# Linear-attention state of a fused kernel: the fade of the old state done on TensorE into PSUM, and the sum copied out by ScalarE

## Chip, core and metric

One Trainium2 chip, one core. The metric is the time of one execution on the device in microseconds (us), as the median of some runs. The reader needs four of the core's engines: PE (TensorE, matrix products into PSUM), DVE (VectorE), ACT (ScalarE) and POOL (GpSimd); SP issues the transfers (DMAs) between HBM and SBUF.

## What is computed

A linear attention with a decaying state, followed by two products with gating and a second block with softmax and normalisation. Only the first part matters here. In the reference, per block of rows and per head:

```python
inter = np.einsum('bhid,bhde->bhie', qb * lam_pow[None], kv_state)
out[:, :, sl] = intra + inter
kb_dec = kb * rev_pow[None]
kv_state = lam_block[None, :, None, None] * kv_state + np.einsum('bhsd,bhse->bhde', kb_dec, vb)
```

The state of a head is 64 x 64. It is faded by one number per head, `lam_block`, and a product of decayed keys and values is added. There are 2 batches, 8 heads, 768 positions, head size 64; then 1536 rows go through 512 x 1536 (twice), 1536 x 512, 512 x 1024 and 1024 x 512.

## The kernel before

The attention runs over 12 chunks of 128 positions, numbered n = 0 to 11: batch n % 2, position n // 2. Chunk n needs the state that chunk n - 2 left (`state[n - B]`, B = 2). Chunks 10 and 11 are the last of their batch, so ten states are made, the first two (n = 0, 1) without an old one.

A state is one SBUF tile of 128 partitions x 4 x 64 in fp32: eight heads as four pairs `a`, head `e` = 0 of a pair in partitions 0 to 63 and head 1 in partitions 64 to 127. `dec` holds the powers of the decay of each head, in the same layout; its last column, `dec[:, :, P - 1]`, is the decay over a whole chunk.

Every step of the work is a Python generator, and every `yield` ends a part of it. The table `ORDER` lists the parts one by one in the order in which they are issued (`T,5` a second time is the second part of `T` for chunk 5), and each engine runs what it is given in that order. So a row of the table sets the place in the queue of every engine that the part uses. The kinds that matter here:

- `A` (`scores`): products of queries and keys (`pss`, L223), then the mask on DVE (`sc`, L228).
- `K`, `Q` (`kdecay`, `qdecay`): decayed keys `kd` (L208) and queries `qd` (L214), on POOL.
- `C` (`products`): eight products of the old state with `qd` (`px`, L238), eight of values with `sc` (L244), and a maximum on DVE (L114).
- `O` (`fade`): POOL multiplies the old state by the decay of the chunk, into a tile `old` (L254).
- `T` (`carry`): first part eight products of `kd` and values into a PSUM bank `pst` (L263); second part a DVE addition of `old` and `pst` into a new state (L269), or, for n = 0 and 1, a copy by ACT (L267).
- `X`, `Y`, `J`: scales and splits of `px` into half-precision pairs (L123 on PE, L131 to L134, L297, L313 on DVE, L293, L319 on ACT).
- `D`, `S`: weights decoded (ACT L340, L344, DVE L346) and split into `wab` (ACT L418, DVE L421).
- `L`, `R`: the first products of the second stage (L143, out `pa`, `pb` and `rA`, `rB`, `rC`).

All PSUM banks come from one ring of eight. Tiles `state` and `old` share a ring of four. The products in fp32 show as two records on PE each, so a set of eight is x16 in the profile.

Of the kernel before, what the change touches and what calls it, by code (L numbers as in the profile page):

```python
# [8 lines left out]
F32 = mybir.dt.float32  # L9
# [8 lines left out]
B, H, S, D = 2, 8, 768, 64  # L18
P = 128
W = 512  # L20
WARM = 22
NP = H // 2
# [7 lines left out]
NJ = W // P  # L30

LAST = 2
ORDER = ("G,qk,0 G,kv,0 G,qk,1 G,ab,0 G,kv,1 G,qk,2 G,kv,2 G,qk,3 G,kv,3 G,ab,1 G,qk,4 G,kv,4 G,qk,5 G,kv,5 A,0 K,0 K,0 A,0 T,0 A,0 C,0 T,0 O,2 A,1 C,0 D,ab,0 "
# [59 lines left out]
def body(ctx: ExitStack, tc, qk, kv, consts, wab, wo, wi, wo2, out):  # L93
    nc = tc.nc
    E = mybir.EngineType
    ctx.enter_context(tc.manual_schedule(engines={E.SP, E.PE, E.DVE, E.Activation, E.Pool}))
    const = ctx.enter_context(tc.tile_pool(name="const", bufs=1))
    sl = ctx.enter_context(tc.tile_pool(name="sl", bufs=1))
# [3 lines left out]
    def bank(nm):  # L102
        return ps.tile([P, W], F32, tag="bank", name=nm)
# [64 lines left out]
    dec = const.tile([P, NP, P], F32, name="dec")  # L168
# [5 lines left out]
    ident = const.tile([P, P], F32, name="ident")  # L174
# [17 lines left out]
    n = 1  # L192
# [2 lines left out]
        n *= 2  # L195


    order = [(g % B, g // B) for g in range(NCH)]
    sc, qd, kd, px, state = {}, {}, {}, {}, {}
    xs, sx, xst, olds = {}, {}, {}, {}  # L200

    def kdecay(n):

# [44 lines left out]
        amax(xst[n // 2][:, n % 2:n % 2 + 1], o)  # L248
        yield

    def fade(n):
        b, c = order[n]
        olds[n] = sl.tile([P, NP, D], F32, tag="state", name="old", bufs=4)
        nc.gpsimd.tensor_mul(olds[n], state[n - B], dec[:, :, P - 1:P].to_broadcast([P, NP, D]))  # L254
        yield

    def carry(n):
        b, c = order[n]
        v = kvs[n][:, 1]
        pst = bank("pst")[:, :NP * D].rearrange("p (a d) -> p a d", a=NP)  # L260
        for a in range(NP):
            for e in range(2):
                nc.tensor.matmul(pst[e * D:(e + 1) * D, a], kd[n][:, 2 * a + e], v[:, 2 * a + e], start=True, stop=True, skip_group_check=True)  # L263
        yield
        new = sl.tile([P, NP, D], F32, tag="state", name="state", bufs=4)
        if c == 0:
            nc.scalar.copy(new, pst)  # L267
        else:
            nc.vector.tensor_add(new, olds[n], pst)  # L269
        state[n] = new  # L270
        yield

# [574 lines left out]
    def load(nm, n):  # L847
# [4 lines left out]
        else:  # L852
            load_w((nm, n))
        yield

    kinds = {"G": load, "A": scores, "K": kdecay, "Q": qdecay, "C": products, "O": fade, "T": carry, "X": scale_x, "Y": split_x,
             "D": decode, "P": scale_w, "p": scale_f, "S": split_w, "J": sums_x, "H": sums_w, "E": split_s, "R": R1, "L": L1, "M": L2, "U": scale_y, "V": split_y, "B": sums_y, "F": split_ys, "I": sums_i, "k": split_si, "N": L3, "n": norm, "Z": Z, "W": L4}
    parts = {}
    for word in ORDER.split():
        if word not in parts:  # L860
# [48 lines left out]
```

## Time and profile before

| | |
|---|---|
| median of 3 runs | 457.61 us (457.37 to 458.52) |
| the profiled execution's own time | 457.83 us |
| its span, first to last instruction | 456.1 us |
| PE busy | 438.5 us of the span |
| DVE, ACT, POOL busy | 337.7, 248.5, 232.2 us |
| granted TensorE clock, mean | 0.981 |

The profile is one execution taken by the hardware profiler. Its time outside the span is 1.73 us. Attention work stands in the first 125 us or so, mixed with the first products of the second stage; from then on PE runs the large products. Three views are used below: the chain of work that ended last, followed back from the last instruction; the timeline, with an engine's idle time before a group in brackets and who ended it; and a table of stretches with the busy time of each engine in each and the granted clock of PE (1.00 is 2.4 GHz, 0.50 is 1.2 GHz).

### The profile page before, as it was taken

The page shows a single profiled execution, that of the slowest core. Times are in us where ns is not written, and L with a number is a line of the kernel's source. Part 1 is how long each engine was busy: PE and PEld are TensorE (multiplying, and loading weights), DVE is VectorE, ACT ScalarE, POOL GpSimd, SP SyncE. Part 2 cuts the span into 40 slices and gives each one's busy share as a digit, 9 for nine tenths or more (in the row PEclk, how much of TensorE's full clock was granted, in tenths as well). Part 3 has the DMA queues.
Part 4 walks back from the last instruction along what each step waited for, and adds up shares of the span by engine and source line. Part 5 has one row for each costly group of instructions (what it writes and reads, how often), then busy time and mean ns, then how long its engine had stood idle before and what let it go on. Part 6 is the DMA issues. An engine that isn't in the chain of part 4 may idle for free.

```text
span 456.1 us, 7817 instructions
## 1 busy us (share of the span) xinstructions
PE 438.5 (96%) x3092; PEld 273.9 (60%) x3092; DVE 337.7 (74%) x571; ACT 248.5 (54%) x397; POOL 232.2 (51%) x259
## 2 busy tenths in 40 slices
PE   6879699999999999999999999999999989999997
PEld 5768565457888886776874444455444434444455
DVE  5798889899887446556699259977986879996830
ACT  2473636677776556556884526756714645534321
POOL 4796534595615652152526247338244794837500
PEclk9879889999999999999999999999999999999999
DMA  8957418552200004340222422020012123344511
GB/s 309 416 200 279 185 59 311 185 184 94 93 1 0 2 1 161 125 177 1 93 92 86 192 96 91 0 94 1 2 23 46 48 38 78 70 115 105 127 47 46
DMA packets 30372, 48.74 MB, mean 107 GB/s; under 512 B 22272, under 2 KB 22528, under 8 KB 27008
## 3 DMA queue, kind: packets, MB, share of 16 engines
q1 hardware_dynamic: 30336, 48.25, 31.2%
q8 instruction: 24, 0.39, 0.4%
q14 instruction: 12, 0.10, 0.1%
HBM read 39.86 MB, written 3.15 MB: 94 GB/s over the span
## 4 chain that ended last, share of the span: by engine, by line
PE 86%; DMA 4%; POOL 4%; DVE 2%; ACT 1%; issue 1%; SPq 0%; ACTq 0%; POOLq 0%
PE py L143 20%; PE rA L143 14%; PE po L143 13%; PE pa L143 7%; PE rB L143 7%; PE pb L143 7%; PE hA L143 5%; DMA qk<-in_qk_dram 4%; PE rC L143 3%; PE hB L143 2%; PE pss L223 2%; PE px L238 2%; PE px L244 1%; PE hC L143 1%; PE pst L263 1%
## 5 line engine op out<-in xcount | busy, mean ns | idle before, releaser
L143 PE MATMUL py<-g,wo 128*128 128x512 f16 x432 | 94.4, 379 | 0.0
L143 PEld LDWEIGHTS <-wab 128*128 128x128 f16 x744 | 72.0, 98 | 36.0 <-issue 0.9
L143 PEld LDWEIGHTS <-wo 128*128 128x128 f16 x432 | 42.1, 98 | 50.5
L143 PE MATMUL po<-wo,zT 128*128 128x512 f16 (+1 forms) x312 | 63.4, 363 | 0.0
L143 PEld LDWEIGHTS <-ws 128*128 128x128 f16 x576 | 56.0, 98 | 7.4 <-DVE ws L452 0.3
L143 PEld LDWEIGHTS <-zT 128*128 128x128 f16 x312 | 30.5, 98 | 31.5
L556 POOL TENSOR_TENSOR g<-c,g 128x512 f16<-128x512 f32 x24 | 31.2, 1318 | 33.9 <-ACT g L554 33.8
L143 PE MATMUL rA<-xt,ws 128*128 128x256 f16 x288 | 35.2, 273 | 0.0
L489 POOL TENSOR_TENSOR g<-asb,g 128x512 f16<-128x512 f32 x12 | 16.0, 1334 | 34.2 <-ACT g L487 34.2
L143 PE MATMUL pa<-xh,wab 128*128 128x512 f16 (+1 forms) x156 | 33.3, 363 | 0.0
L143 PE MATMUL pb<-xh,wab 128*128 128x512 f16 (+1 forms) x156 | 33.2, 363 | 0.0
L512 ACT ACTIVATE p<-rA 128x512 f32<-128x512 f32 x36 | 21.2, 595 | 20.6 <-PE rA L143 20.6
L800 POOL TENSOR_TENSOR zr<-e,zr 128x512 f16<-128x512 f32 x20 | 24.7, 1255 | 12.0 <-ACT zr L796 12.0
L344 ACT ACTIVATE raw<-raw 128x1024 f32<-128x1024 f32 x26 | 29.4, 1141 | 0.0
L841 ACT ACTIVATE ob<-po,glm 128x512 f32<-128x512 f32 (+1 forms) x13 | 8.4, 654 | 36.2 <-PE po L143 30.4
L545 POOL TENSOR_TENSOR c<-p,p 128x512 f32<-128x512 f32 x12 | 15.7, 1306 | 20.6 <-ACT p L512 19.5
L143 PEld LDWEIGHTS <-yt 128*128 128x128 f16 x144 | 14.0, 98 | 16.9 <-DVE yt L644 0.3
L550 DVE SCALAR_TENSOR_TENSOR c<-c 128x512 f32<-128x512 f32 x24 | 20.1, 847 | 4.9 <-ACT c L547 4.6
L346 DVE SCALAR_TENSOR_TENSOR fab<-raw,fab 128x1024 uint32<-128x1024 uint32 x12 | 15.5, 1294 | 7.4 <-ACT raw L344 7.4
L418 ACT ACTIVATE wab<-fab,sab 128x512 f16<-128x512 f32 (+1 forms) x24 | 14.4, 640 | 11.0 <-DVE sab L134 11.0
L421 DVE SCALAR_TENSOR_TENSOR wab<-fab,sab,wab 128x512 f16<-128x512 f32 (+1 forms) x24 | 18.9, 822 | 1.1 <-ACT wab L418 1.1
L796 ACT CAST zr<-e 128x512 f16<-128x512 f32 x20 | 11.4, 616 | 14.2 <-DVE e L785 14.2
(167 smaller groups left out, 902.3 us busy)
## 6 DMA issues: line engine op xcount, KB each, us to landing
raw<-in_wab_dram SPq DMA_DIRECT2D x12, 1024.0 KB, 5.5
raw<-in_wo_dram SPq DMA_DIRECT2D x10, 1024.0 KB, 4.8
qk<-in_qk_dram SPq DMA_DIRECT2D x12, 512.0 KB, 9.1
kv<-in_kv_dram SPq DMA_DIRECT2D x12, 512.0 KB, 9.9
raw<-in_wi_dram SPq DMA_DIRECT2D x4, 1024.0 KB, 5.5
out_dram<-ob SPq DMA_DIRECT2D x11, 256.0 KB, 2.0
zT<-zr SPq DMA_TRANSPOSE x20, 3.1
out_dram<-ob SPq DMA_DIRECT2D x2, 128.0 KB, 1.7
```

What stands on the lines that cost most here:

```text
L143: nc.tensor.matmul(o, w[a], x[b], start=start and i == 0, stop=stop and i == 2, skip_group_check=True)
L344: nc.scalar.activation(hi.bitcast(F32), hi.bitcast(F32), AF.Prelu, scale=2.0 ** -112, alpha=2.0 ** 32)
L346: nc.vector.scalar_tensor_tensor(out=flat, in0=hi, scalar=3, in1=flat, op0=ALU.logical_shift_left, op1=ALU.bitwise_or)
L418: nc.scalar.activation(w[:, z, 0, c], src[:, z, c], AF.Copy, scale=ss[:, z:z + 1])
L421: nc.vector.scalar_tensor_tensor(out=w[:, z, 1, c], in0=src[:, z, c], scalar=ss[:, z:z + 1], in1=w[:, z, 0, c], op0=ALU.mult, op1=ALU.subt ...
L489: nc.gpsimd.tensor_sub(g[:, 1], a, g[:, 0])
L512: nc.scalar.activation(r, o, AF.Copy, scale=2.0 ** -28)
L545: nc.gpsimd.tensor_sub(c1[:, 1], p167, p5)
L550: nc.vector.scalar_tensor_tensor(out=c[:, :, 0], in0=c[:, :, 0], scalar=2.0, in1=c[:, :, 1], op0=ALU.mult, op1=ALU.mult)
L556: nc.gpsimd.tensor_sub(g[:, 1], c[:, :, 0], g[:, 0])
L796: nc.scalar.copy(rows[0][:, z * W:(z + 1) * W], e[z])
L800: nc.gpsimd.tensor_sub(lo, e[z], hi)
```

## The change

The step `O` is gone, with its eight entries in `ORDER` and its tiles `old`. In its place a constant tile `fades` is made once, by two POOL instructions after `dec`: for every head a 64 x 64 diagonal matrix with the decay of the chunk on the diagonal. In the second part of `T`, for n = 2 to 9, eight products of this diagonal with the old state are added to `pst` in PSUM; then ACT copies the sum into the new state, where DVE added before. All other entries of `ORDER` keep their sequence.

```diff
+    fades = const.tile([P, NP, D], F32, name="fades")
+    for e in range(2):
+        r = slice(e * D, (e + 1) * D)
+        nc.gpsimd.tensor_mul(fades[r], ident[r, e * D:(e + 1) * D].rearrange("p (a d) -> p a d", a=1).to_broadcast([D, NP, D]), dec[r, :, P - 1:P].to_broadcast([D, NP, D]))
...
-    def fade(n):
-        b, c = order[n]
-        olds[n] = sl.tile([P, NP, D], F32, tag="state", name="old", bufs=4)
-        nc.gpsimd.tensor_mul(olds[n], state[n - B], dec[:, :, P - 1:P].to_broadcast([P, NP, D]))
-        yield
...
-                nc.tensor.matmul(pst[e * D:(e + 1) * D, a], kd[n][:, 2 * a + e], v[:, 2 * a + e], start=True, stop=True, skip_group_check=True)
+                nc.tensor.matmul(pst[e * D:(e + 1) * D, a], kd[n][:, 2 * a + e], v[:, 2 * a + e], start=(a == 0), stop=c == 0, skip_group_check=True)
         yield
         new = sl.tile([P, NP, D], F32, tag="state", name="state", bufs=4)
-        if c == 0:
-            nc.scalar.copy(new, pst)
-        else:
-            nc.vector.tensor_add(new, olds[n], pst)
+        if c:
+            for a in range(NP):
+                for e in range(2):
+                    r = slice(e * D, (e + 1) * D)
+                    nc.tensor.matmul(pst[r, a], fades[r, a], state[n - B][r, a], start=False, stop=True, skip_group_check=True)
+        nc.scalar.copy(new, pst)
```

PE's queue where chunks 5 and 4 are begun (scores of chunk 5, then the old states times `qd` of both; `-` before, `+` now, line numbers have shifted):

```order
 L263 MATMUL pst<-kv,kd 64x64 x16
-L223 MATMUL pss<-qk 128x128 x8
-L238 MATMUL px<-qd,state 64x128 x16
+L229 MATMUL pss<-qk 128x128 x8
+L270 MATMUL pst<-state,fades 64x64 x16
+L244 MATMUL px<-qd,state 64x128 x16
 L143 LDWEIGHTS wab
 L143 MATMUL pa<-xh,wab 128x2x128
```

Two sets of eight products (chunks 3 and 2) now stand between the scores and the first products that read those states. Two more sets (chunks 5 and 4) stand some 48 rows on, after the first halves of `pa` and `pb`; one (chunk 6) stands just ahead of the next `px`, two (7 and 8) each right behind a block of `pa`, and one (9) behind a block of `rB`.

ACT's queue at the same place, before:

```order
L340 ACTIVATE fab<-raw 128x1024
L344 ACTIVATE raw<-raw 128x1024
L418 ACTIVATE wab<-fab,sab 128x512 x2
L482 ACTIVATE asb<-pa 128x512
L487 CAST g<-asb 128x512
```

and now:

```order
L342 ACTIVATE fab<-raw 128x1024
L346 ACTIVATE raw<-raw 128x1024
L271 COPY state<-pst 128x256 x2
L420 ACTIVATE wab<-fab,sab 128x512 x2
L271 COPY state<-pst 128x256 x2
L484 ACTIVATE asb<-pa 128x512
```

The copies of states 3 and 2 stand ahead of the two casts that make `wab`, and those of 5 and 4 ahead of `asb`. On DVE the eight additions are gone and on POOL the eight multiplications; the queue of SP reads the same in both kernels.

## Rows read from the trace of the kernel before

**Rows 1.** The chain that ended last, some pieces: start us, us, what.

```profile
8.44 13.18 DMA qk<-in_qk_dram
...
26.85 1.97 PE pst L263 x30
...
31.25 2.50 PE px L238 x32
33.75 1.42 PE pa L143 x12
...
44.15 1.10 PE pss L223 x15
...
54.81 1.97 PE px L238 x16
...
125.11 2.62 PE rA L143 x24
```

**Rows 2.** Busy time by stretch: us, each engine (instructions), granted clock, DMA share, GB/s.

```profile
27.00:45.00 18.00, 18.00 (x222) 16.12 (x222) 16.07 (x28) 8.35 (x11) 14.59 (x15) 0.85 0.50 196
50.20:54.80 4.60, 0.38 (x3) 0.14 (x3) 4.53 (x13) 3.15 (x6) 3.27 (x3) 0.80 0.11 43
60.00:350.00 290.00, 290.00 (x1978) 183.69 (x1975) 217.75 (x337) 174.53 (x267) 134.22 (x111) 1.00 0.24 86
350.00:375.00 25.00, 23.55 (x110) 10.58 (x109) 19.50 (x38) 14.47 (x25) 20.36 (x25) 1.00 0.20 43
```

**Rows 3.** The same table for the stretches with PE's clock at half.

```profile
12.00:15.40 3.40, 3.06 (x26) 2.76 (x28) 2.04 (x2) 1.09 (x2) 3.04 (x3) 0.50 1.04 425
25.70:32.40 6.70, 6.03 (x60) 5.50 (x62) 6.53 (x18) 6.20 (x10) 6.54 (x8) 0.50 0.39 156
53.00:59.70 6.70, 5.13 (x52) 4.37 (x52) 6.49 (x17) 3.17 (x7) 6.54 (x9) 0.50 0.02 4
```

**Rows 4.** PE's timeline in three places: start us, us, engine, line, operation, xcount.

```profile
22.22 1.10 PE L263 MATMUL pst<-kv,kd 128*64 128x64 f32 x32
23.25 0.29 PE L123 MATMUL pm<-identb,xst 128*128 128x128 bf16 x2
...
66.42 1.09 PE L238 MATMUL px<-qd,state 64*64 64x128 f32 x16
67.44 1.10 PE L244 MATMUL px<-sc,kv 128*64 128x128 f32 x16
...
115.31 1.47 PE L143 MATMUL rB<-xt,ws 128*128 128x256 f16 x12
116.71 0.69 PE L263 MATMUL pst<-kv,kd 128*64 128x64 f32 x16
117.33 0.29 PE L123 MATMUL pm<-identb,r 128*128 128x128 bf16 x2
```

**Rows 5.** Groups by line, 0 to 140 us: xcount | busy us, mean ns | idle before.

```profile
L254 POOL TENSOR_TENSOR old<-state,dec 128x256 f32<-128x256 f32 x8 | 5.4, 674 | 4.9 <-DVE pm L133 2.4 <-ACT state L267 2.3 <-POOL qd L214 0.2
...
L267 ACT COPY state<-pst 128x256 f32<-128x256 f32 x2 | 0.7, 372 | 12.4 <-PE pst L263 12.4
```

**Rows 6.** Timeline of ACT, DVE and SP, 30 to 39 us.

```profile
30.94 1.32 ACT L418 ACTIVATE wab<-fab,sab 128x512 f16<-128x512 f32 x2
31.82 1.80 DVE L421 SCALAR_TENSOR_TENSOR wab<-fab,sab,wab 128x512 f16<-128x512 f32 x2
34.99 1.42 DVE L346 SCALAR_TENSOR_TENSOR fab<-raw,fab 128x1024 uint32<-128x1024 uint32 x1
36.47 0.33 SPq L163 DMA_DIRECT2D raw<-in_wab_dram  x1
37.58 1.22 DVE L346 SCALAR_TENSOR_TENSOR fab<-raw,fab 128x1024 uint32<-128x1024 uint32 x1
```

**Rows 7.** Timeline of PE and DVE, 52 to 55 us.

```profile
52.87 0.36 PE L123 MATMUL pm<-identb,xst 128*128 128x128 bf16 x2 [2.66 <-DVE xst L114]
54.25 0.41 DVE L269 TENSOR_TENSOR state<-old,pst 128x256 f32<-128x256 f32 x1
```

More of the change, by code (lines that the diff above doesn't have):

```diff
@@ L32 @@
 LAST = 2
-ORDER = ("G,qk,0 G,kv,0 G,qk,1 G,ab,0 G,kv,1 G,qk,2 G,kv,2 G,qk,3 G,kv,3 G,ab,1 G,qk,4 G,kv,4 G,qk,5 G,kv,5 A,0 K,0 K,0 A,0 T,0 A,0 C,0 T,0 O,2 A,1 C,0 D,ab,0 "
[1 row of a table removed]
+ORDER = ("G,qk,0 G,kv,0 G,qk,1 G,ab,0 G,kv,1 G,qk,2 G,kv,2 G,qk,3 G,kv,3 G,ab,1 G,qk,4 G,kv,4 G,qk,5 G,kv,5 A,0 K,0 K,0 A,0 T,0 A,0 C,0 T,0 A,1 C,0 D,ab,0 "
[1 row of a table added]
          "X,0 C,2 Y,0 C,3 J,0 Y,0 Q,4 Y,1 T,3 C,3 D,ab,1 T,2 J,0 X,1 K,4 X,1 D,ab,1 K,4 X,1 J,0 Q,5 Y,2 J,0 J,1 Y,2 K,5 Y,3 J,0 J,0 K,5 J,1 J,0 J,0 J,1 T,5 J,1 "
[5 rows of a table removed]
[5 rows of a table added]
          "C,9 D,ab,3 T,8 D,ab,4 X,4 L,0,2 L,0,2 D,ab,5 X,4 G,ab,6 X,4 Q,10 D,ab,4 Y,8 J,4 p,1 p,3 C,10 L,0,2 D,ab,5 p,1 A,10 p,3 Q,11 L,0,2 p,1 p,3 S,ab,1 Y,8 "
@@ L195, in body @@
         n *= 2
+    fades = const.tile([P, NP, D], F32, name="fades")
+    for e in range(2):
+        r = slice(e * D, (e + 1) * D)
+        nc.gpsimd.tensor_mul(fades[r], ident[r, e * D:(e + 1) * D].rearrange("p (a d) -> p a d", a=1).to_broadcast([D, NP, D]), dec[r, :, P - 1:P].to_broadcast([D, NP, D]))
     order = [(g % B, g // B) for g in range(NCH)]
     sc, qd, kd, px, state = {}, {}, {}, {}, {}
-    xs, sx, xst, olds = {}, {}, {}, {}
+    xs, sx, xst = {}, {}, {}
     def kdecay(n):
@@ L854, in load @@
         yield
-    kinds = {"G": load, "A": scores, "K": kdecay, "Q": qdecay, "C": products, "O": fade, "T": carry, "X": scale_x, "Y": split_x,
+    kinds = {"G": load, "A": scores, "K": kdecay, "Q": qdecay, "C": products, "T": carry, "X": scale_x, "Y": split_x,
              "D": decode, "P": scale_w, "p": scale_f, "S": split_w, "J": sums_x, "H": sums_w, "E": split_s, "R": R1, "L": L1, "M": L2, "U": scale_y, "V": split_y, "B": sums_y, "F": split_ys, "I": sums_i, "k": split_si, "N": L3, "n": norm, "Z": Z, "W": L4}
```

12 rows, old and new, of the table ORDER are left out of this document.

## The prediction

> **What bounds the kernel now.** I read the chain of work that ended last first, then the table of stretches, then the timelines. From 60 to 350 us PE is busy for all of 290.00 us, and from 350 to 375 for 23.55 of 25 [rows 2]: what is put into PE's queue there, or ahead of it, moves the end. Only what falls into a wait of PE ahead of 60 us can be hidden, so that is where the reader has to look. Up to 21.62 us the chain is the landing of the `qk` transfers [rows 1]. From 27 to 45 us PE is busy for 18.00 of 18.00 us, and the chain is PE's own queue to 45.25. Then other engines have it: between 50.2 and 54.8 PE works for 0.38 us and DVE for 4.53 [rows 2]. This part was begun by PE's last `pss` at 44.15 [rows 1], so if PE comes there later, it starts later. From 54.81, where `px` starts, PE is never short of work again but for the 1.45 us around 373.
>
> So of the eight places where fades enter PE's queue, four (chunks 3, 2, 5, 4) lie in a full stretch that a DVE and ACT stretch follows, one (chunk 6) in PE's long wait, and three (7, 8, 9) in the full stretch behind 60 us.
>
> **What goes.** Eight POOL multiplications of 0.67 us [rows 5] and eight DVE additions of 0.41 us [rows 7]. POOL and DVE gate none of the places above but one: the addition at 54.25 releases `px` at 54.81 [rows 1, 7]. Their time elsewhere is worth nothing unless DVE is the bound, which is a rival below. Eight ACT copies of 0.37 us [rows 5] come in; ACT works 8.35 us of the 18 in the full stretch [rows 2], so the copies cost by what they wait for, not by their length. The two POOL instructions that build `fades` are about 1.2 us by the same row of POOL; they hold up the first `kd`, but until 21.62 us everything waits for `qk`, which covers them. Without that cover they would cost the 1.2.
>
> **The price of one set of fades.** The trace has no product of 64 columns in this tile shape. The nearest are the `pst` sets: as many products, 64 columns, weights of 128 x 64. Two in a row take 22.22 to 23.25, 0.52 each; one alone takes 116.71 to 117.33, 0.62, or 0.69 from its first start to its last end [rows 4]. The other neighbour has the same 64 x 64 weights but 128 columns: 66.42 to 67.44, 1.02 [rows 4]. I take 0.62, since columns are what must differ between the two, and 0.52 and 0.69 as the bounds; 1.02 is a rival. A set among half-precision products also delays the first of it: the `rB` block ahead of it takes 1.40 from 115.31 to 116.71 [rows 4], where two blocks of that kind in a row take 2.62, 1.31 each [rows 1]: so 0.09 more, 0.71 in all. At half clock thirty records take 1.97 [rows 1], so a set of sixteen takes 1.05.
>
> A rule would make a set cheaper. The Trainium skill, page "TensorE: Matmul & The Clock Gate", section "Back-to-back issue gap", puts products of up to 64 columns at a floor of about 25 ns from start to start. Sixteen of them would be an estimated 0.40 us, and the sum below would come to about 3.3 us. The trace does not agree for the like sets: 0.62 for sixteen is 39 ns each.
>
> **Chunks 3 and 2.** PE reaches them at 31.25 at half clock; by the table the clock is half until 32.4 at least and full in the stretch after, and I put the rise at 32.47. The first set ends at 32.30. Of the second a sixth is done by 32.47, and the rest takes 0.52 at full clock: 32.99. The two `px` sets follow at full clock, 2 x 1.02, to 35.03, where `pa` starts now at 33.75. The states are there in time: the copy of state 3 runs beside the second set, that of state 2 beside the first `px`. Loss 1.28.
>
> The same place has the new wait. On ACT the copies stand ahead of the casts of `wab`, which ran at 30.94, long before they were needed [rows 6]. Now ACT holds them until the second set has left PE: 32.99 and 0.37 of copy, 0.66 for the cast (half of 1.32), 0.90 on DVE (half of 1.80) is 34.9, and PE wants `wab` at 35.03. It just fits. Behind it on DVE stand the second `wab` step (to 35.8), a mask and then the decode now at 34.99, which so starts some 1.5 later; SP's load at 36.47, which waits for that decode [rows 6], and the loads queued behind it go out 1.5 later too. Their data come 1.5 later to a PE that is by then 2.4 later, so that costs nothing. The two `pst` banks are held until the copies; in the ring of eight the next to want them are the second `px` and `pa`, both later than the copies.
>
> **Chunks 5 and 4.** Two sets in a row inside the first `pa` and `pb`: 1.03 and 0.09, 1.12. Up to 45 us that is 2.40, and the stretch from 45.25 to 54.81 moves back by as much.
>
> **Chunk 6.** The set stands behind the `pm` at 52.87, while PE waits [rows 7]. Started at 53.1 at half clock it ends at 54.15; with 0.37 of copy and twice the 0.15 that lie now between the addition's end at 54.66 and `px` at 54.81, `px` could start at 54.8, as it does now. At full clock it would be 0.4 earlier; if ACT is late by half a copy, 0.2 later. I take 0.
>
> **Chunks 7, 8, 9.** 3 x 0.71 = 2.13, all on PE's full stretch. Copies 7 and 8 sit ahead of `asb` and a `wab` cast on ACT, which then wait for the fade, some 1 us; a block of 2.6 us stands on PE before anything reads these.
>
> **Sum.** 1.28 + 1.12 + 0 + 2.13 = 4.53. Against the profiled execution, 457.83, that is 462.4. That one is 0.22 over the median of the runs, so I give 462.1. With 0.52 or 0.69 for a set the sum is 3.8 or 5.1.
>
> **Rivals.**
>
> *The clock turns at other moments.* The granted clock was half from 25.7 to 32.4 and from 53.0 to 59.7, but earlier only from 12.0 to 15.4 [rows 3]. PE falls idle and comes back some 2.4 us later now, and its last low stretch may come out as the short kind, or as much longer. A `px` set takes 1.02 at full clock [rows 4] and 1.97 at half [rows 1], so 3.4 us at half clock lose about 1.7: 460.4 or 463.8. Nothing in the profile says which.
>
> *ACT's queue holds `wab` back.* The fit above has 0.1 to spare. If PE's second set ends 0.5 later, all at half clock, or DVE is still at something else when the cast is done, `pa` waits: 0.3 to 1.0 more, 462.8 in the middle.
>
> *A set costs what its tile shape cost with 128 columns*, 1.02 (1.97 at half clock [rows 1]): first place 2.2, second 2.1, chunk 6 about 0.4, and 3 x 1.11 behind: 8.0, 465.6. The `L244` set with full 128-row weights also takes 1.03 for 128 columns, which speaks for columns and against shape.
>
> *DVE is the bound up to 54.81* (not slower). DVE is busy for 16.07 of the 18 us and for 4.53 of 4.60 [rows 2]. If the release of 54.81 hangs on DVE's queue from 30 us on and not on PE's `pss` at 44.15, then the four fades ahead of it are hidden, and four additions less, 4 x 0.41, bring it 1.64 forward. With 2.13 behind, that is 0.5: 458.1. It decides if DVE has no idle time in that stretch; but it had 1.9 us from 27 to 45 [rows 2], and the chain goes from PE to DVE at 45.25 [rows 1].
> The Trainium skill, page "SBUF — State Buffer", section "SBUF: two separate sides", says that DVE and GpSimd exclude each other on a shared port for a whole instruction, which would make the loss of POOL's work worth more to DVE. Here the decode on DVE took 1.42 at 34.99 and 1.22 at 37.58 [rows 6], so 0.2 each and not a whole POOL instruction.
>
> **How the numbers follow.** Chances: the sum as it stands 0.55; the clock 0.12 short and 0.08 long; ACT's queue 0.12; 1.02 a set 0.05; DVE 0.08. A measurement of this kernel can tell about 0.3%, 1.4 us, from no change. The DVE case is within that, with a little of it faster (0.02); the short clock with cheap sets comes to 459.7, just outside, so 0.02 of it may lie within, and 0.01 is left for a gain not seen. So faster 0.03, within 0.08, slower 0.89. The range leaves out the DVE case and the dear set, 0.13, and a little at both ends: below, the short clock with sets of 0.52, 459.7; above, the long clock with sets of 0.69, 464.4.
>
> **What would show it.** In the trace after: the fade sets at 0.6 us each from start to start, 1.0 at half clock; `pa` at 35.0 where it was 33.75, with no gap ahead of it; the last `pss` of the stretch at 46.5, and `px` at 57.2; PE gapless from there. It is wrong if PE shows a wait ahead of `pa`, if `px` of chunk 8 still starts at about 54.8, or if the low stretches of the clock differ in length.

## The result

The changed kernel takes 462.64 us (median; 462.39 to 462.98) and the kernel before 457.51 us. The ratio is 1.011, with a 95% interval of 1.0077 to 1.0142: the change costs some 5 us. 462.1 was predicted, with 459.7 to 464.4 as the range. The total was right, and so were the prices of PE's sets of fades; but one term that had been set to nothing cost more than 1 us, and in the profile three smaller gains covered it up.

### The profile page after: what moved, and what is told of

It is laid out like the page before. It is cut to its first block, busy times and chain, and to the rows that moved or that the text cites. A ratio compares the mean times of both kernels' runs of the same rounds, so it can differ in the third digit from the quotient of the medians.

```text
span 460.6 us, 8069 instructions
## 1 busy us (share of the span) xinstructions
PE 445.0 (97%) x3220; PEld 279.0 (61%) x3220; DVE 334.2 (73%) x563; ACT 251.1 (55%) x405; POOL 226.5 (49%) x253
## 4 chain that ended last, share of the span: by engine, by line
PE 89%; POOL 4%; DVE 3%; issue 1%; ACT 1%; DMA 0%; ACTq 0%; DVEq 0%; POOLq 0%
PE py L143 20%; PE rA L143 14%; PE po L143 12%; PE pa L143 7%; PE rB L143 7%; PE pb L143 7%; PE hA L143 5%; PE rC L143 3%; PE pss L229 3%; PE px L250 2%; PE hB L143 2%; PE px L244 2%; PE hC L143 1%; PE pst L270 1%; PE pst L263 1%
## 5 line engine op out<-in xcount | busy, mean ns | idle before, releaser
L271 ACT COPY state<-pst 128x256 f32<-128x256 f32 x10 | 3.7, 372 | 32.2 <-PE pst L270 16.7
L423 DVE SCALAR_TENSOR_TENSOR wab<-fab,sab,wab 128x512 f16<-128x512 f32 (+1 forms) x24 | 17.8, 780 | 4.6 <-ACT wab L420 4.6
L229 PE MATMUL pss<-qk 64*128 64x128 f32 x192 | 18.1, 335 | 1.2 <-DVE tt L315 0.6
```

The source lines that it names most:

```text
L229: nc.tensor.matmul(pss[e][:, a * P:(a + 1) * P], t[r, 1, a], t[r, 0, a], start=True, stop=True, skip_group_check=True)
L423: nc.vector.scalar_tensor_tensor(out=w[:, z, 1, c], in0=src[:, z, c], scalar=ss[:, z:z + 1], in1=w[:, z, 0, c], op0=ALU.mult, op1=ALU.subt ...
```

## The profile after

The table of stretches, in the columns of [rows 2], for the two stretches at half clock and the full one behind 61 us:

```profile
27.40:34.00 6.60, 5.96 (x74) 5.26 (x72) 4.77 (x13) 4.67 (x7) 6.04 (x6) 0.50 0.21 84
...
58.10:61.30 3.20, 3.20 (x31) 2.87 (x27) 2.80 (x8) 2.27 (x6) 2.71 (x6) 0.50 0.01 3
61.50:350.00 288.50, 288.50 (x2027) 184.29 (x2026) 214.39 (x330) 172.69 (x264) 135.67 (x111) 1.00 0.24 87
```

PE is as full behind 61 us as it was [rows 2]: nothing that comes late there can be caught up. The last low stretch of the clock goes from 58.1 to 61.3 us here, where it went from 53.0 to 59.7 before [rows 3].

To see where the 4.5 us of span went (456.1 to 460.6), follow PE's first start at seven places. PE's timeline before:

```profile
31.18 2.57 PE L238 MATMUL px<-qd,state 64*64 64x128 f32 x32
33.68 1.48 PE L143 MATMUL pa<-xh,wab 128*128 128x256 f16 x12
...
44.08 1.16 PE L223 MATMUL pss<-qk 64*128 64x128 f32 x16
...
54.81 1.97 PE L238 MATMUL px<-qd,state 64*64 64x128 f32 x16 [1.57 <-DVE state L269]
...
74.09 1.09 PE L238 MATMUL px<-qd,state 64*64 64x128 f32 x16
...
121.58 1.09 PE L238 MATMUL px<-qd,state 64*64 64x128 f32 x16
```

PE's timeline after (L270 are the fades, L244 is now `px` from the state):

```profile
32.19 1.97 PE L270 MATMUL pst<-state,fades 64*64 64x64 f32 x32
33.95 2.00 PE L244 MATMUL px<-qd,state 64*64 64x128 f32 x32
35.88 1.48 PE L143 MATMUL pa<-xh,wab 128*128 128x256 f16 x12
...
38.61 1.15 PE L270 MATMUL pst<-state,fades 64*64 64x64 f32 x32
39.69 1.48 PE L143 MATMUL pa<-xh,wab 128*128 128x256 f16 x12
...
47.47 1.16 PE L229 MATMUL pss<-qk 64*128 64x128 f32 x16
...
57.79 1.80 PE L244 MATMUL px<-qd,state 64*64 64x128 f32 x16 [0.57 <-DVE sx L134]
...
66.48 0.68 PE L270 MATMUL pst<-state,fades 64*64 64x64 f32 x16
67.09 2.76 PE L143 MATMUL pb<-xh,wab 128*128 128x512 f16 x12
69.78 1.09 PE L244 MATMUL px<-qd,state 64*64 64x128 f32 x16
...
78.17 1.09 PE L244 MATMUL px<-qd,state 64*64 64x128 f32 x16
...
126.11 1.09 PE L244 MATMUL px<-qd,state 64*64 64x128 f32 x16
```

The first `px` start of chunk 9 before is at 66.42 [rows 4]. The lag at each place, and what the stretch up to it added:

| place | before | after | lag | added | predicted |
|---|---|---|---|---|---|
| behind the scores of chunk 5 | 31.18 | 32.19 | 1.01 | 1.01 | 0 |
| `pa` (sets of chunks 3, 2) | 33.68 | 35.88 | 2.20 | 1.19 | 1.28 |
| last `pss` (sets 5, 4) | 44.08 | 47.47 | 3.39 | 1.19 | 1.12 |
| `px` of chunk 8 (set 6) | 54.81 | 57.79 | 2.98 | -0.41 | 0 |
| `px` of chunk 9 (set 7) | 66.42 | 69.78 | 3.36 | 0.38 | 0.71 |
| `px` of chunk 10 (set 8) | 74.09 | 78.17 | 4.08 | 0.72 | 0.71 |
| `px` of chunk 11 (set 9) | 121.58 | 126.11 | 4.53 | 0.45 | 0.71 |

From there both kernels take 334.5 us to the end. A set takes 0.61 from start to start (66.48 to 67.09), two in a row 1.08 (38.61 to 39.69), against 0.62 and 1.03 in the prediction, which adds 0.09 for the block ahead of them. The step that failed is in the first line.

What makes the first line begins at the start of the program. POOL's timeline after, against a first `kd` at 5.96 before:

```profile
5.93 1.29 POOL L201 TENSOR_TENSOR fades<-ident,dec 64x256 f32<-64x256 f32 x2
7.30 1.20 POOL L214 TENSOR_TENSOR kd<-kv,mask 128x256 f32<-128x256 f32 x2
```

DVE's timeline, the mask of chunk 1 and the first decode, before and then after:

```profile
9.89 1.29 DVE L228 TENSOR_TENSOR sc<-pss,mask 128x512 f32<-128x512 f32 x2 [0.39 <-PE pss L223]
13.12 1.44 DVE L346 SCALAR_TENSOR_TENSOR fab<-raw,fab 128x1024 uint32<-128x1024 uint32 x1 [1.94 <-ACT raw L344]
```

```profile
13.41 1.29 DVE L234 TENSOR_TENSOR sc<-pss,mask 128x512 f32<-128x512 f32 x2 [1.31 <-PE pss L229]
14.62 1.68 DVE L348 SCALAR_TENSOR_TENSOR fab<-raw,fab 128x1024 uint32<-128x1024 uint32 x1
```

Before, DVE stood idle for 1.94 us and began the decode when ACT was done. After, the mask of chunk 1, which follows the first `kd` and `pst` through PE, came 3.5 us later than its 9.89 and pushed the decode to 14.62, 1.50 later. From there up to 31 us DVE had three gaps before, of 0.82, 0.31 and 0.47 us; after, the first is gone, and DVE stays 1.0 behind. So in this profile DVE's queue carries the lag to PE, beside the landing of `qk` that the prediction had looked at alone. But the mask is 3.5 us late, and `kd` only 1.3: the rest is PE's, whose first sets take longer here, as told next.

## Experiments

Theory F: a set of fades costs its own length where PE is short of time, and nothing where PE waits. Theory S: the build of the diagonals, ahead of the first `kd` on POOL, costs more than 1 us through DVE's queue. Rival to S, theory C: the lag at the start came from PE's clock, by chance of the execution. The sets of `pss` up to 13 us took 2.08 us in the profile after and 1.16 later. 2.08 is the length of such a set at half clock (56.71 before), though the column of the granted clock reads 1.00 up to 13.6; so a low clock there is worked out from the lengths and not read from a row. Further rivals: relief of DVE and POOL, and ACT's queue.

**The build moved behind the first `kd`.**

```diff
     for e in range(2):
         nc.gpsimd.tensor_mul(d4[:, :, e], k4[:, :, e], ...)
+        if n == 0 and e == 1:
+            build()
```

`build` issues the two POOL instructions.

> The changed kernel, with the two POOL instructions that build the diagonals issued behind the first two decayed-key multiplications, in POOL's pause, instead of ahead of them. In the changed kernel's trace the first `kd` started at 7.30 us against 5.96 before and everything from 13 us on ran about 1.0 us late. Theory S (the build on POOL ahead of the first `kd` set DVE's whole queue back): first `kd` at about 6.0, the scores of chunk 5 reach PE about 1.0 earlier, and the time falls from 462.6 to about 461.6. Theory C (that 1.0 came from PE's clock, which was at half until 13.6 us in that execution and not in the one of before): `kd` earlier, but the stretch from 13 to 31 us hardly moves, time 462.3 to 462.7. The prediction's own step (the transfers cover the build): 462.6, nothing gained.

Measured: 461.07 us, ratio to before 1.0084 (1.0063 to 1.0104). POOL's timeline:

```profile
6.11 1.20 POOL L216 TENSOR_TENSOR kd<-kv,mask 128x256 f32<-128x256 f32 x2 [0.29 <-DMA kv<-in_kv_dram]
7.27 1.31 POOL L203 TENSOR_TENSOR fades<-ident,dec 64x256 f32<-64x256 f32 x2
```

The first `kd` waits for its data again and the build lies in a pause. As theory S said, the fades behind the scores of chunk 5 start 1.09 earlier (31.10, after 32.19). The profiled execution, at 462.97 the slowest of six, loses that again: its low stretch lies later, so that `px` runs at half clock, and `pa` starts at 35.89. The median is 1.57 lower. Since an execution of one kernel differs from the next by as much, the pair was run again on one chip:

> The changed kernel once more, beside the next one on the same chip. Theory S: 462.6, and 1.0 to 1.6 more than the next one. Theory C (no loss at the start): the same as the next one within 0.4.

> The changed kernel with the build of the diagonals moved into POOL's pause, once more. Theory S: 461.1, some 1.0 to 1.6 less than the one before it. Theory C: the same as the one before it within 0.4.

Measured: the changed kernel 463.24 us (461.97 to 465.60), with the build moved 461.46 (460.77 to 462.64): 1.78 between them.

**The build alone, in the kernel before.**

```diff
+    fades = const.tile([P, NP, D], F32, name="fades")
+    for e in range(2):
...
```

The rest is as in the change.

> The kernel before with only the two POOL instructions that build the diagonals added ahead of the first `kd`; nothing reads them. Theory S: about 1.0 us slower, 458.5. Theory C and the prediction's step (covered by the transfers): 457.5, within 0.3.

Measured: 458.98 us, 1.0042 (1.0022 to 1.0061), 1.46 over the median of before. Three comparisons agree: two POOL instructions of 1.3 us together cost about 1.5 us. That much of theory S holds: a chance of the clock alone would hardly fall the same way three times. It shows in the traces too. The `pst` sets that start at 22.22 before [rows 4] start between 20.98 and 22.20 in the nine other traces without a build ahead of `kd`, and later in all four traces with one: at 23.22 after, at 24.29 with the copies on DVE (below), and here, first with the build alone and then in the changed kernel's second run:

```profile
22.33 1.10 PE L269 MATMUL pst<-kv,kd 128*64 128x64 f32 x32
25.80 1.10 PE L263 MATMUL pst<-kv,kd 128*64 128x64 f32 x32
```

That the cost goes through DVE's queue is not shown. In the trace of the build alone `kd` is as late (7.22) and the decode starts at 13.73, yet PE is back to 0.11 behind at 22.33 (that execution took 458.37, less than the median). How large the lag is goes with how long PE's first sets stay long: the last `pss` set of 2.08 us starts at 10.42 with the build alone, at 11.30 after, and at 16.52 in the second run, where the lag is 3.58. In no trace without the early build does a `pss` set that starts between 8 and 13 us take 2.08; they take 1.16 to 1.78. So a late `kd` may also keep PE slow for longer, and theories S and C need not exclude each other; no run parts the two ways.

**Only the last three chunks on PE**, the others as before.

```diff
+ON_PE = (7, 8, 9)
...
+        if n in ON_PE:
...
+        if c == 0 or n in ON_PE:
             nc.scalar.copy(new, pst)
```

> Only chunks 7, 8 and 9 are faded on PE and copied by ACT; chunks 2 to 6 keep POOL and DVE, and the diagonals are built in POOL's pause behind the first `kd`. Theory F (a set in PE's full stretch costs its own length): 3 x 0.71 = 2.1 us, 459.6. Rival (the copies in ACT's queue or the two changes of tile shape cost more than the products): 460.3 or more. Rival (DVE and POOL relief is worth something behind 60 us): 459.0 or less.

Measured: 459.96 us, 1.0056 (1.0033 to 1.0080), 2.4 over before. 2.1 lies within the interval, and so does the rival's 460.3; the profile speaks against that one, for a set again takes 0.61 from start to start:

```profile
62.36 0.68 PE L283 MATMUL pst<-state,fades 64*64 64x64 f32 x16
62.97 2.76 PE L144 MATMUL pb<-xh,wab 128*128 128x512 f16 x12
```

**Only the first four on PE**: the same with `ON_PE = (2, 3, 4, 5)`.

> Only chunks 2, 3, 4 and 5 are faded on PE and copied by ACT; chunks 6 to 9 keep POOL and DVE, diagonals built in POOL's pause. Theory F: 1.28 for the first two and 1.12 for the others, 2.4 us, 459.9, give or take 1.7 by where the low clock stretches fall; `pa` starts some 1.3 later than before, the last `pss` of the stretch 2.4 later. Rival (DVE is the bound up to 55 us, so sets on PE are hidden and four additions less help): 457.5 or less, `px` of chunk 8 at 54.8 or earlier. Rival (the casts of `wab` held on ACT): 460.5 and a gap on PE ahead of `pa`.

Measured: 459.41 us, 1.0041 (1.0024 to 1.0057), 1.9 over before. In its profile `pa` starts at 34.27 and the last `pss` at 45.86, 0.6 and 1.8 later than before, with no gap on PE ahead of `pa`. The sets began at 30.79, 0.4 earlier than `px` did before, so they added 1.0 and 1.2. DVE as the bound falls: `px` of chunk 8 starts at 56.64, not at 54.8.

```profile
56.64 1.97 PE L249 MATMUL px<-qd,state 64*64 64x128 f32 x16 [1.65 <-DVE state L287]
```

**The sets left out altogether**, and the build with them: what the change takes off POOL and DVE, by itself. The old state is then missing from the new one.

```diff
-        if c:
...
         nc.scalar.copy(new, pst)
```

> The changed kernel without the eight sets and without the build of the diagonals: ACT copies `pst` alone, so the old state is left out of the new one. What is left of the change is its relief: no POOL multiplication, no DVE addition, eight ACT copies. Theory F: relief is worth nothing, 457.5, within 0.5. Rival (relief of DVE is worth something up to 55 us): 456.5 or less. Rival (ACT's copies cost by themselves): 458.2 or more.

Measured: 457.39 us, 0.9999 (0.9978 to 1.0019). Eight POOL multiplications and eight DVE additions fewer, with eight ACT copies more, change nothing that the interval, some 0.9 us either way, can show.

**The copies on DVE**, not ACT.

```diff
-        nc.scalar.copy(new, pst)
+        if c:
+            nc.vector.tensor_copy(new, pst)
+        else:
+            nc.scalar.copy(new, pst)
```

> The changed kernel, but DVE copies the eight sums out of PSUM, not ACT. Theory F and S (PE's sets and the early build are the whole loss; ACT's queue just fits): 462.6, within 0.4, and `pa` starts at the same place behind the `px` sets. Rival (the casts of `wab` are held back by the copies on ACT): DVE's copies set them free, 0.3 to 1.0 less, 461.6 to 462.3. Rival (DVE is what bounds up to 31 us): eight copies more on DVE make it slower, 463.2 or more.

Measured: 466.39 us, 1.0212 (1.0176 to 1.0248), 3.75 over the changed kernel. None of the numbers allowed for that much; the direction is the one given for DVE as a bound. Rows of DVE's, SP's and PE's timelines:

```profile
34.41 0.42 DVE L272 COPY state<-pst 128x256 f32<-128x256 f32 x1 [1.70 <-PE pst L270]
...
41.63 0.89 DVE L272 COPY state<-pst 128x256 f32<-128x256 f32 x2 [3.42 <-PE pst L270]
42.44 1.22 DVE L351 SCALAR_TENSOR_TENSOR fab<-raw,fab 128x1024 uint32<-128x1024 uint32 x1
```

```profile
43.73 0.33 SPq L163 DMA_DIRECT2D raw<-in_wab_dram  x1
```

```profile
51.33 1.16 PE L229 MATMUL pss<-qk 64*128 64x128 f32 x16 [1.50 <-DMA qk<-in_qk_dram]
```

It is not the length of the copies, which is 0.42. DVE waits for PE's sets, 1.70 and 3.42 us, and the decode queued behind the copies waits with it; SP's load waits for the decode, 43.73 where it was 36.47 [rows 6]; and PE then waits 1.50 for `qk`. With 0.26 more for `qk` at 56.38, and 0.82 and 0.73 for DVE at 104.70 and 114.53, PE waits 3.3 us in places where the changed kernel's PE has no wait. (The profiled execution, 470.01, is the slowest of the six; its start is 1.07 later than the changed kernel's by the `pst` sets above, so not all of its lag comes from the copies.) In the changed kernel the copies wait on ACT, whose next work is not due, DVE's decode comes in time, and SP issues at 38.46:

```profile
33.36 0.37 ACT L271 COPY state<-pst 128x256 f32<-128x256 f32 x1 [1.30 <-PE pst L270]
34.21 0.37 ACT L271 COPY state<-pst 128x256 f32<-128x256 f32 x1 [0.48 <-PE pst L270]
34.48 1.33 ACT L420 ACTIVATE wab<-fab,sab 128x512 f16<-128x512 f32 x2
```

```profile
35.24 1.41 DVE L423 SCALAR_TENSOR_TENSOR wab<-fab,sab,wab 128x512 f16<-128x512 f32 x2 [2.66 <-ACT wab L420]
...
37.17 1.21 DVE L348 SCALAR_TENSOR_TENSOR fab<-raw,fab 128x1024 uint32<-128x1024 uint32 x1
```

The casts of `wab` on ACT are held until 34.48 (30.94 before, [rows 6]); their second half on DVE starts at 35.24, and PE takes up `pa` at 35.88 straight behind `px`, with no gap. The fit of the prediction held.

**Dead sets in the kernel before.** POOL's and DVE's fade stay; eight sets with a zero matrix are added to `pst` in the eight places of PE's queue.

```diff
+        nc.gpsimd.memset(fades, 0.0)
...
+        if n in ON_PE:
...
         if c == 0:
             nc.scalar.copy(new, pst)
         else:
             nc.vector.tensor_add(new, olds[n], pst)
```

> The kernel before, with POOL's and DVE's fade kept as they are, and eight sets of products of a zero matrix with the old state added to PSUM in the same eight places of PE's queue (the zero matrix is set by one memset in POOL's pause). Only PE's work is added; nothing is relieved and ACT copies nothing more. Theory F (the loss is PE's work alone, relief is worth nothing): as the changed kernel with the build moved, 461.1, within 0.5. Rival (POOL and DVE relief of the change gives back x): slower than 461.1 by x, so 462 or more if relief is worth 1 us.

Measured: 464.25 us, 1.0146 (1.0120 to 1.0173). By the expectation, relief would be worth 3 us; but with no sets at all it was worth nothing. I had overlooked that the addition on DVE must now wait for PE's set, which is the mechanism above; PE then waits for `qk` here too:

```profile
47.77 1.16 PE L232 MATMUL pss<-qk 64*128 64x128 f32 x16 [1.75 <-DMA qk<-in_qk_dram]
```

To part the two, the dead sets were written to the other half of the bank:

```diff
-        pst = bank("pst")[:, :NP * D].rearrange("p (a d) -> p a d", a=NP)
+        two = bank("pst").rearrange("p (z a d) -> p z a d", z=2, a=NP)
+        pst, spare = two[:, 0], two[:, 1]
```

> The kernel before, POOL's and DVE's fade as they are, with eight dead sets of products in the eight places of PE's queue (zero matrix, set by a memset), but written to the other half of the PSUM bank, where nothing reads them: DVE's addition needn't wait for them. Theory W (the dead sets in `pst` itself gave 464.3, 3.2 over the changed kernel with the build moved, because DVE's additions, and all that is queued behind them, waited for PE's sets): without that wait as the changed kernel with the build moved, 461.1, within 0.7. Rival (POOL's and DVE's relief is worth 3 us in the changed kernel): 464 again. It is not relief by the kernel without sets, which was at 457.4, so I expect the first.

Measured: 467.43 us, 1.0206 (1.0162 to 1.0250). The run does not part them, for the wait stayed: DVE's addition still waits for PE's dead set (L280), though that set is written to the other half. DVE and PE:

```profile
32.11 0.42 DVE L284 TENSOR_TENSOR state<-old,pst 128x256 f32<-128x256 f32 x1 [1.77 <-PE pst L280]
```

```profile
48.70 1.16 PE L232 MATMUL pss<-qk 64*128 64x128 f32 x16 [1.60 <-DMA qk<-in_qk_dram]
```

It is the chain of the copies on DVE once more. Why it cost 3 us more than the dead sets in `pst` itself is not settled; the two ran on different chips, and their low stretches of the clock fell differently.

**The sets of chunks 3 and 2 in PE's wait**, ahead of `pst` of chunks 5 and 4, with the build moved. The second part of `T` is cut in two, fades and copy, and the fades come earlier in the table.

```diff
+            yield
         nc.scalar.copy(new, pst)
...
-T,2 J,0 X,1 K,4
+T,2 J,0 X,1 T,3 T,2 K,4
```

> The changed kernel with the build moved behind the first `kd`, and with the two sets of chunks 3 and 2 issued ahead of the `pst` products of chunks 5 and 4, where PE waits some 2 us for `kd` (24.5 to 26.4 us); their copies stay where they are in ACT's queue. Theory F (a set costs only where PE is short of time): these two sets cost nothing, 1.1 to 1.3 less than with the build alone moved, 459.8 to 460.0. Rival (a set costs wherever it stands, by PE's clock or the following waits): 461.1.

Measured: 461.14 us, 1.0073 (1.0049 to 1.0097). Theory F had said 459.8 to 460.0, and the rival 461.1. It is no less than with the build alone moved (461.07, on another chip); but intervals of 0.0048 and 0.0041 of the ratio, some 2 us each, can't tell 1.2 us, so this median decides nothing. PE's timeline shows the sets hidden up to `pa`; first this kernel, then the one without any sets:

```profile
22.60 1.15 PE L257 MATMUL pst<-state,fades 64*64 64x64 f32 x32
25.98 0.33 PE L250 MATMUL pst<-kv,kd 128*64 128x64 f32 x2 [2.22 <-POOL kd L199]
...
34.10 1.50 PE L126 MATMUL pa<-xh,wab 128*128 128x256 f16 x12
```

```profile
25.79 0.33 PE L259 MATMUL pst<-kv,kd 128*64 128x64 f32 x2 [3.23 <-POOL kd L210]
...
33.99 1.48 PE L143 MATMUL pa<-xh,wab 128*128 128x256 f16 x12
```

PE's wait is 2.22 in place of 3.23, and `pa` comes at 34.10 and 33.99, at like clocks.

**Only the sets that can be hidden**: chunks 3 and 2 in that wait, chunk 6 in the wait ahead of 55 us, all others on POOL and DVE (`ON_PE = (2, 3, 6)`). The base is the kernel before, of which there are more runs.

> Only chunks 2, 3 and 6 are faded on PE: the sets of 3 and 2 in PE's wait ahead of 26 us, that of 6 in its wait ahead of 55 us; the other five chunks keep POOL and DVE; diagonals built in POOL's pause. Theory F (a set costs nothing where PE waits): 457.5, within 0.5. Rival (a set costs wherever it stands): 3 x 0.6 more, 459.3.

Measured: 457.70 us, 0.9997 (0.9970 to 1.0023). The rival's 459.3 (1.0038) lies outside the interval, which leaves room for 1 us at most. Theory F holds within that: three sets in waits cost nothing that can be measured. PE's timeline:

```profile
23.45 1.15 PE L266 MATMUL pst<-state,fades 64*64 64x64 f32 x32
26.24 0.33 PE L259 MATMUL pst<-kv,kd 128*64 128x64 f32 x2 [1.64 <-POOL kd L200]
...
31.33 1.96 PE L232 MATMUL px<-qd,state 64*64 64x128 f32 x32 [1.02 <-ACT state L269]
...
50.68 1.16 PE L217 MATMUL pss<-qk 64*128 64x128 f32 x16 [1.73 <-DMA qk<-in_qk_dram]
...
53.13 0.68 PE L266 MATMUL pst<-state,fades 64*64 64x64 f32 x16
54.39 1.09 PE L232 MATMUL px<-qd,state 64*64 64x128 f32 x16 [0.57 <-DVE sx L118]
```

Not all is free in this order: PE waits 1.02 at 31.33 for ACT's copy of a state.

No version here beats the kernel before: what the change relieves is worth nothing, and only three of the eight sets were hidden; for the other five no other place was tried.

## Why the prediction was right, point by point

- **What bounds the kernel.** Right: PE full from the first `px` of chunk 8 on, and each set ahead of that either in PE's full stretch or in a wait. The sets left out give 457.39, the three in waits 457.70.
- **The price of a set.** Right: 0.61 alone and 1.08 for two, against 0.62 and 1.03. 0.61 for sixteen records is 38 ns each, so the cheaper set of 0.40 did not come either. At half clock two took 1.76 (32.19 to 33.95), 0.88 each, where 1.05 was worked out from `pst`. The rival of 1.02 falls.
- **Chunks 3, 2, 5, 4.** Right: 2.38 against 2.40, though two differences cancel in it: both sets of chunks 3 and 2 ran at half clock, not one and a sixth, and each was cheaper than the 1.05. The order of the first steps was as told, `pa` straight behind `px`; it stood at 35.88 and not at 35.0, as the start was late by 1.01.
- **The build of the diagonals.** Wrong. The step said that the transfers up to 21.62 us cover it, and set it to nothing. In three comparisons it costs 1.46, 1.57 and 1.78. The chain that ended last named only `qk`; it doesn't show how little other engines lag behind. DVE's first decode had 1.94 us to spare, and in the profile after a `kd` 1.3 late, with PE's first sets at 2.08 us, used this up. Whether DVE's queue or PE's slow first sets make the cost stays open.
- **Chunk 6.** Sized 0, measured -0.41. The clock was full at the set here, for which the prediction named 0.4; the new state also no longer stands in DVE's queue behind the small operations for the scale. ACT's copy ends at 57.69; the profile puts the last of PE's wait to the scale `sx` on DVE, which ends at 57.78.
- **Chunks 7, 8, 9.** Set 8 is 0.72, as worked out. With set 7 the clock's short low stretch gives 0.33 back, the short case of the first rival. In set 9's stretch two blocks of `rB` take 1.31 where they took 1.47 and 1.42 before, 0.27 less; before, PE's weight loads waited there for `ws` from DVE, so a little relief does show in this profile. The group of these loads on the page (busy us, mean ns, idle before and its releaser), before and then after:

```profile
L143 PEld LDWEIGHTS <-ws 128*128 128x128 f16 x576 | 56.0, 98 | 7.4 <-DVE ws L452 0.3
```

```profile
L143 PEld LDWEIGHTS <-ws 128*128 128x128 f16 x576 | 56.2, 98 | 7.0
```

- **The rivals.** DVE as the bound up to 54.81 fell as it was told (no gain from additions taken off DVE), but the runs showed its other side: DVE's queue has no room for a wait. ACT's queue held `wab` back by 3.5 us and cost nothing. The loss of POOL's work was worth nothing to DVE that shows (457.39 without the sets). The 0.2 us by which one decode was longer, which the prediction set against a whole POOL instruction, could be the rest of one and decides nothing. Low stretches of other lengths were a named sign of being wrong, and the last one is 3.2 us in place of 6.7; what it gave back is in the two points above. `px` of chunk 8 stood at 57.79 and not at 57.2, with the late start in it.
- **The sum.** 4.53 was predicted and 4.53 is PE's lag at the last place, by chance: 1.01 too little at the start, and 0.41, 0.33 and 0.26 too much behind it. The medians say the same in other sizes: with the build moved the sets cost 3.55 and 3.88 (461.07 against 457.52, 461.46 against 457.58), and the early build the rest.

## What to carry to other kernels

Work that moves to the engine that bounds the kernel costs its length wherever that engine is full, however cheap it is; count its places one by one, and only those in a wait are free (three sets in waits: 457.70 against 457.58; eight sets, with their build: 5 us more). For a result that must be fetched behind such work, choose the engine by what is queued behind the fetch, not by who is faster: the same copy cost nothing on ACT and 3.75 us on DVE, through a decode, a load and back to PE. And that the chain names a transfer does not mean that it covers a setup step at the start: look at what every engine does with a late result. Here 1.3 us on POOL became 1.5 us at the end.

## What the runs showed of the hardware

One kernel's executions spread more than the three shown at first: 17 of the kernel before, on one chip, lie between 455.48 and 460.56 us. The profiles show stretches with the granted clock at 0.50 at other moments, and not always of one length: 25.7 to 32.4 and 53.0 to 59.7 us before [rows 3], 27.4 to 34.0 and 58.1 to 61.3 after. The execution of the kernel with the three hidden sets shows none from 20 us to the end of its work, and yet takes 457.96: PE then waits 1.73 us for `qk` at 50.68, which the kernel before and the changed one don't do there, and 1.02 for ACT at 31.33; so part of what the full clock gains is lost in waits.

Products of the same count and tile shape with half the columns took 0.61 us against 1.02 at full clock (0.54 each where two sets stand in a row), and, two in a row, 0.88 each against 1.90 at half (54.81 to 56.71, before).

At the start of the program PE's sets stay long for very different times: the last `pss` set of 2.08 us there starts at 4.69 in one trace (the dead sets) and at 16.52 in another (the changed kernel's second run).
